# A three-part fp32 network on one core: weight blocks summed on VectorE, their parts stored as they are decoded, low halves taken one operation later, output stores on ScalarE's queue

## The chip, the cores and the metric

One Trainium2 chip, one of its cores. The engines are TensorE (PE; its weight loads PEld), VectorE (DVE), ScalarE (ACT), GpSimd (POOL) and SyncE (SP), which here only issues transfers. The metric is the device time of one execution in microseconds (us).

## The reference

With N = 3072 tokens of width 384, three parts run one after the other, all in fp32:

```python
state = alpha * state + outer(k_t, v_t); y_t = q_t @ state      # 4 x 8 heads, 768 steps
x = y as 3072 x 384
for tokens with x @ w_skip > 0: x += gate * (max(x @ w1[e], 0) @ w2[e])   # one of 8 experts
h = maximum(maximum(x @ w1, x @ w2), x @ w3)                    # 3 x (384 -> 768)
out = h @ w_out                                                 # 768 -> 384
```

## The kernel before

All fp32 products run as three matmuls of halves: each number is split in a high half h and a low half l = t - h, and the product is hh + hl + lh (fp32r operands). The change lies in the last part, the dense stage, which starts 299.7 us into the profiled execution, and in how its weights are made ready while the experts run.

**Decoding.** The four weights of the dense stage arrive as 64-bit words in 12 units of 128x768 (weight w, third u, in the order `ORDER`). `mdecs` decodes a unit on ACT (L98) and DVE (L108, L109, L102, L103, in place in a buffer `dt`), casts the high half `mh` on ACT (L612) and subtracts the low half `ml` (L615) on POOL for the first seven units, on DVE for the others. The last units, the u = 2 thirds of w = 0, 1, 2, are decoded in the first rounds of the dense stage.

**Token groups.** The tokens stand in six groups of 512. Groups 0 and 1 are computed directly, in six rounds each, f = 0 to 5 (128 columns of the hidden layer): `gemm1(g, f)` is 27 matmuls of 128x512 into three banks; ACT copies the first bank to `hf` (L841), DVE takes the maximum with the two others (L844), ACT casts the high half (`hb0h`/`hb1h`) and POOL subtracts the low half (`hb0l`/`hb1l`). `gemm2` of the round before (12 matmuls of 128x384) follows. Its last round copies four banks to `ob` on ACT (L862, a ring of three) and stores each (L863).

**Jobs.** The other four groups use a scheme of 15 block products in place of 18, for which sums of weight blocks and of token blocks are needed. `sums(w)` adds mh + ml back into whole blocks `tb` on POOL (L874, 128x768) and stores the parts of seven single blocks (`ONE`) as they are to the scratch `wd` in DRAM (L877). `wjobs` makes 13 combinations of blocks on DVE (L882), casts the high half of eight of them on ACT (L888), subtracts the low half on DVE (L889) and stores both to `wd` (L890). `xjobs(s)` transposes the token groups (`xg`, loaded by L815, transposed on PE at L820, copied to `temps` by ACT, L920/L997), makes 12 combinations on DVE (L906 to L910), and 15 high and low halves (L927 on ACT; L928 on POOL for the six of `XPOOL`, else on DVE). `pump(g, f, n)` emits the next n jobs behind a bank, so that jobs and rounds share the engines' queues:

```python
                if w == 0:
                    A.copy(t, ph)
                    pump(g, f, 2)
                else:
                    V.tensor_tensor(t, ph, t, ALU.max)
                    pump(g, f, 1)
```

**Steps.** Then two passes s = 0, 1 follow, each of six `step`s of 15 products (L970 to L972, 45 matmuls of 128x512) with weights reloaded from `wd` (`wdload`, L955 and L956), and a round of `outs2` and `store`, beside which the token blocks of the second pass are made.

**Order.** Each engine runs its instructions in the order of the program. Loads of `xg`, stores to `wd` and stores of the output all stand in SP's queue, in that order too: an issue that waits holds all behind it.

Of the kernel before, what the change touches and what calls it, by code (L numbers as in the profile page):

```python
# [55 lines left out]
GT = 512  # L56
# [3 lines left out]
LOADAT = 4  # L60
# [11 lines left out]
XSEQ = ((3, (2, 0), 1, (2, 1), 1), (6, (1, 0), 1, (2, 0), 1), (0, (0, 0), 1, 6, 1), 0, (9, 0, 1, (2, 1), 1), 9,  # L72
# [3 lines left out]
XPOOL = (7, 13, 3, 14, 2, 6)  # L76
# [5 lines left out]
def tile_gla_moe_moe2(ctx, tc, akq, vp, rp, wgt, cst, io, ew, md, out):  # L82
# [37 lines left out]
    with tc.manual_schedule():  # L120
# [465 lines left out]

        def mload(i):
            rm[i] = rmp.tile([128, 2 * UN], F32, name="rm")
            w, u = ORDER[i]
            SY.dma_start(out=rm[i].bitcast(I32), in_=md[3 * w + u].bitcast(I32))  # L590

        def mdecs():

            ts = {}

            def begin(i):
                if i < len(ORDER):
                    if i + 1 < len(ORDER):
                        mload(i + 1)
# [203 lines left out]
        wd = tc.dram_tile([nf2, 128, NR * 256], F32, name="wd")  # L803
        wv = wd.rearrange("f p (r t c) -> r p f t c", r=NR, t=2)
# [17 lines left out]
        def gemm1(g, f):  # L822
# [13 lines left out]
            for w in range(3):  # L836
# [12 lines left out]
        def gemm2(g, f):  # L849
# [4 lines left out]
            for c in range(4):  # L854
# [14 lines left out]
        mv = lambda m, w, k: m[w].rearrange("p (f k c) -> k p f c", f=nf2, k=k3)[k]  # L869
        fv = lambda a: a.rearrange("p (f c) -> p f c", f=nf2)  # L870
# [41 lines left out]
        def xjobs(s):  # L912
            reads = lambda j: [XONE.get(j, j)] if isinstance(j, int) else [j[1], j[3]]
            last = {v: i for i, j in enumerate(XSEQ) for v in reads(j)}
            free, at = list(temps), {}
            for k, n in ((1, 0), (2, 0), (2, 1), (0, 0), (0, 1), (1, 1)):
# [4 lines left out]
                if s == 0:  # L921
                    yield
            for i, j in enumerate(XSEQ):
                src = [at[v] for v in reads(j)]
                free[:0] = [at.pop(v) for v in reads(j) if last[v] == i]
# [8 lines left out]
                yield  # L934
# [6 lines left out]
        jobs = alljobs()  # L941
# [35 lines left out]
        def step(i):  # L977
# [26 lines left out]
            if i:  # L1004
                wdload(i + 1)
            neg(t5, p("A", 7))
            next(tail, None)
# [9 lines left out]
            sub(t3, p("D", 4))  # L1017
            lmax(t3, t1)
            add(t2, p("A", 5))
# [5 lines left out]
            def rest():  # L1025
                V.scalar_tensor_tensor(t2, p("A", 12), -1.0, t2, ALU.mult, ALU.max)
# [16 lines left out]
        def store(s, n, c, po, last=False):  # L1043
# [5 lines left out]
            else:  # L1049
                ends["A"] = A.copy(o, po)  # L1050
            ends["S"] = SY.dma_start(out=out[r0:r0 + 128, :], in_=o)

        pend = None
        for g in range(ng):
            for f in range(nf2):
# [3 lines left out]
                if g == 0:  # L1059
# [4 lines left out]
                    if 1 <= f < 4:  # L1064
                        sums(f - 1)
# [15 lines left out]
        gemm2(*pend)  # L1081
        wdload(1)
# [247 lines left out]
```

## Time and profile before

| | us |
|---|---|
| median of 3 runs (lowest, highest) | 622.01 (621.72, 623.18) |
| profiled execution, its own time | 624.9 |
| span of its profile | 623.1 |
| PE busy | 578.6 (93%) |
| DVE busy | 454.9 (73%) |
| ACT busy | 295.3 (47%) |
| POOL busy | 281.3 (45%) |
| mean granted TensorE clock, share of full | 0.976 |

The trace is of one execution. Times in its rows are microseconds from the span's start. Durations in a timeline overlap the next start a little, since an engine starts the next instruction before the last has fully ended; the distance of two starts is what one costs in a row. "[3.81 <-DVE xhl L118]" is idle time of the engine just before the instruction, and what ended it.

### The profile page before, as it was taken

To read this page: it belongs to the slowest core of one execution; us is meant where nothing else is said; L and a number is where in the kernel's file an instruction comes from. 1 tells how busy PE (TensorE), PEld (TensorE's weight loads), DVE (VectorE), ACT (ScalarE), POOL (GpSimd) and SP (SyncE) were. 2 spreads that over 40 slices of the span, in tenths; PEclk is the share of its full clock that TensorE was granted. 3 is DMA by queue.
4 is the path that set the end of the run, shared out by engine and by line. 5 is a ranking of instruction groups with operands and counts; after the bars stand their busy time and mean duration, and the time that the engine had idled before them with its cause. 6 is when DMAs were issued, how large, how long until landed. Compare 5 with 4: busy or idle time off the path is not lost. (4 is left out here: it accounts for less than half of the span.)

```text
span 623.1 us, 10650 instructions
## 1 busy us (share of the span) xinstructions
PE 578.6 (93%) x3995; PEld 510.4 (82%) x3995; DVE 454.9 (73%) x726; ACT 295.3 (47%) x593; POOL 281.3 (45%) x223
## 2 busy tenths in 40 slices
PE   7999999979999999999997975997999998999996
PEld 4888888869899999999786864786777798777795
DVE  7899999956898889898698953365676856686710
ACT  3555575644666666663323233244445355535411
POOL 6453788534355655543267310153445324445310
PEclk9999999999999999999997996998999999999999
DMA  8789997733768766744087267202846441746011
GB/s 326 290 244 329 318 337 267 292 117 116 271 256 300 246 237 230 277 180 170 27 268 230 102 213 275 94 2 72 332 158 220 138 157 42 275 145 228 7 53 56
DMA packets 50524, 123.03 MB, mean 197 GB/s; under 512 B 4098, under 2 KB 38384, under 8 KB 46880
## 3 DMA queue, kind: packets, MB, share of 16 engines
q1 hardware_dynamic: 47904, 117.43, 54.5%
q0 software_dynamic: 2560, 4.83, 2.0%
q8 instruction: 33, 0.54, 0.3%
q14 instruction: 27, 0.22, 0.1%
HBM read 93.03 MB, written 32.28 MB: 201 GB/s over the span
## 5 line engine op out<-in xcount | busy, mean ns | idle before, releaser
L118 POOL TENSOR_TENSOR wl<-raw,wh 128x768 fp32r<-128x768 f32 x26 | 51.1, 1964 | 57.4 <-ACT wh L117 57.3
L118 DVE TENSOR_TENSOR wl<-raw,wh 128x768 fp32r<-128x768 f32 x38 | 56.3, 1481 | 10.4 <-ACT wh L117 10.4
L117 ACT CAST wh<-raw 128x768 fp32r<-128x768 f32 x64 | 53.4, 835 | 19.7 <-PE po L665 15.5
L645 PE MATMUL ph<-xh,wh 128*128 128x256 f32 x192 | 56.4, 294 | 0.6 <-DVE hl L651 0.5
L646 PE MATMUL ph<-xl,wh 128*128 128x256 f32 x192 | 54.4, 284 | 0.4 <-DVE xl L118 0.3
L647 PE MATMUL ph<-xh,wl 128*128 128x256 f32 x192 | 54.4, 283 | 0.0
L665 PE MATMUL po<-wh,hl 128*128 128x384 f32 x128 | 43.4, 339 | 1.2 <-DVE hl L651 1.2
L663 PE MATMUL po<-wh,hh 128*128 128x384 f32 x128 | 43.5, 340 | 0.0
L664 PE MATMUL po<-wl,hh 128*128 128x384 f32 x128 | 43.1, 337 | 0.0
L225 POOL TENSOR_TENSOR k<-akq,sf 128x512 f32<-128x512 f32 x24 | 28.5, 1186 | 24.5 <-DVE sf L222 16.0
L265 PE MATMUL ps<-q,k 64*128 64x128 f32 x384 | 32.1, 287 | 7.9 <-POOL q L240 3.4
L416 POOL DMA_INDIRECT slots<-xr,si x24 | 24.3, 1014 | 30.7 <-DVE xr L413 15.5
L645 PEld LDWEIGHTS ph<-xh,wh 128*128 128x128 f32 x192 | 36.6, 190 | 1.5 <-DVE hl L651 1.3
L646 PEld LDWEIGHTS ph<-xl,wh 128*128 128x128 f32 x192 | 36.4, 190 | 0.8 <-DVE xl L118 0.5
L265 PEld LDWEIGHTS ps<-q,k 64*128 64x128 f32 x384 | 26.4, 188 | 12.3 <-issue 4.8
L647 PEld LDWEIGHTS ph<-xh,wl 128*128 128x128 f32 x192 | 36.4, 189 | 0.0
L271 DVE TENSOR_TENSOR sm<-ps,cs 128x512 f32<-128x512 f32 x48 | 30.3, 674 | 3.5 <-remote 3.1
L651 DVE SCALAR_TENSOR_TENSOR hl<-ph,hh 128x256 fp32r<-128x256 f32 x64 | 26.2, 416 | 8.1 <-ACT hh L650 6.9
L236 DVE TENSOR_TENSOR_SCAN ap<-akq,pcs 128x521 f32<-128x521 f32 x24 | 29.8, 1241 | 2.2
L222 DVE TENSOR_TENSOR_SCAN sf<-akq,pcs 128x520 f32<-128x520 f32 x24 | 29.4, 1224 | 2.5 <-DMA akq<-in_akq_dram 2.2
L650 ACT ACTIVATE hh<-ph 128x256 fp32r<-128x256 f32 x64 | 24.6, 385 | 13.5 <-PE ph L647 12.2
L240 POOL TENSOR_TENSOR q<-akq,ap 128x512 f32<-128x512 f32 x24 | 28.4, 1183 | 4.9 <-DVE ap L236 2.9
(659 smaller groups left out, 1786.1 us busy)
## 6 DMA issues: line engine op xcount, KB each, us to landing
raw<-in_ew_dram SPq DMA_DIRECT2D x15, 1536.0 KB
akq<-in_akq_dram SPq DMA_DIRECT2D x22, 772.5 KB
rm<-in_md_dram SPq DMA_DIRECT2D x12, 768.0 KB
mh<-wd SPq DMA_DIRECT2D x7, 1024.0 KB
ml<-wd SPq DMA_DIRECT2D x7, 896.0 KB
raw<-wd SPq DMA_DIRECT2D x6, 1024.0 KB
raw<-wd SPq DMA_DIRECT2D x6, 896.0 KB
vt<-in_vp_dram SPq DMA_DIRECT2D x24, 200.0 KB
```

The lines of the kernel that those rows point to most:

```text
L117: A.copy(h, src)
L118: (eng or V).tensor_tensor(l, src, h.bitcast(F32), ALU.subtract)
L222: V.tensor_tensor_scan(sf[:, KW - 2::-1], al[:, KW - 1:0:-1], eb[:, KW - 1:0:-1], 0.0, ALU.mult, ALU.max)
L236: V.tensor_tensor_scan(ap, al, eb, 0.0, ALU.mult, ALU.max)
L265: T.matmul(ps[i][:, p, :], kh[j][r0:r0 + 64, p, :], qh[j][r0:r0 + 64, p, :], start=True, stop=True)
L271: V.tensor_tensor(t, fr[j][i], cmask[:, None, :].to_broadcast([128, NP, C]), ALU.mult)
L645: T.matmul(ph, wh[:, z], xh_[e][:, k, :], start=(k == 0), stop=False)
L646: T.matmul(ph, wh[:, z], xl_[e][:, k, :], start=False, stop=False)
L647: T.matmul(ph, wl[:, z], xh_[e][:, k, :], start=False, stop=(k == k3 - 1))
L663: T.matmul(po, hh[:, zm], wh, start=(f == 0), stop=False)
L664: T.matmul(po, hh[:, zm], wl, start=False, stop=False)
L665: T.matmul(po, hl[:, zm], wh, start=False, stop=(f == nf1 - 1))
```

## The change

1. `sums` runs on DVE, on two thirds of each block (128x512); the last third is copied by ACT out of the decode buffer when that third is decoded. It is a job (`yield`) like the others.
2. The parts of the seven `ONE` blocks are stored in thirds by `mdecs`, right behind the subtraction that makes the low half: 42 stores of 128x2x128 in place of 14 of 128x6x128, most of them during the experts.
3. Low halves, of weight combinations and of token blocks, are taken one operation (or more) after the cast of their high half, all on DVE; `XPOOL` is gone.
4. `pump` takes a time in place of a count: each job yields a cost, and jobs are emitted until the amount is spent.
5. Stores of the output go to ACT's queue, but for the last.
6. `wdload(0)` comes a round earlier; `gemm2` of the last round stands inside the first step, behind its fourth product; `add(t2, p("A", 5))` stands ahead of `lmax(t3, t1)` in each step.

```diff
-LOADAT = 4
+LOADAT = 3
+PUMP = (2.0, 1.3, 1.3, 2.0)
...
-XPOOL = (7, 13, 3, 14, 2, 6)
...
                 (G if i < EARLY else V).tensor_tensor(l, t, h.bitcast(F32), ALU.subtract)
+                for k in range(k3 if w < 3 else 0):
+                    if (w, k) in ONE:
+                        for j, m in enumerate((mh, ml)):
+                            SY.dma_start(out=wv[ONE[w, k]][:, 2 * u:2 * u + 2, j],
+                                         in_=mv(m[w], k)[:, 2 * u:2 * u + 2].bitcast(F32))
+                    if u == 2:
+                        A.copy(fv(blk[w, k])[:, 4:], t.rearrange("p (f k c) -> k p f c", f=2, k=k3)[k])
                 yield
...
                 if w == 0:
                     A.copy(t, ph)
-                    pump(g, f, 2)
+                    pump(PUMP[0] if g or f > 3 else 0.7)
                 else:
                     V.tensor_tensor(t, ph, t, ALU.max)
-                    pump(g, f, 1)
+                    pump(PUMP[w] if g or f > 3 else 0.7)
...
-                    SY.dma_start(out=out[g * GT + c * 128:g * GT + (c + 1) * 128, :], in_=o)
-
-        blk = {}
+                    A.dma_start(out=out[g * GT + c * 128:g * GT + (c + 1) * 128, :], in_=o)
+
...
-        def sums(w):
-            for k in range(k3):
-                G.tensor_tensor(fv(blk[w, k]), mv(mh, w, k).bitcast(F32), mv(ml, w, k).bitcast(F32), ALU.add)
-                if (w, k) in ONE:
-                    for t, m in enumerate((mh, ml)):
-                        SY.dma_start(out=wv[ONE[w, k]][:, :, t], in_=mv(m, w, k).bitcast(F32))
+        def sums():
+            for w, k in TORD:
+                V.tensor_tensor(fv(blk[w, k])[:, 0:4], mv(mh[w], k)[:, 0:4].bitcast(F32),
+                                mv(ml[w], k)[:, 0:4].bitcast(F32), ALU.add)
+                yield 0.7
 
         def wjobs():
-            ncl = 0
+            ncl, rest = 0, []
+
+            def low():
+                d, cl, r = rest.pop()
+                V.tensor_tensor(rs_(cl[:, :, 1]), fv(blk[d]), cl[:, :, 0], ALU.subtract)
+                SY.dma_start(out=wv[r], in_=cl)
+
             for d, a, op, b, r in WSEQ:
                 V.tensor_tensor(blk[d], blk[a], blk[b], op)
-                yield
-                if r is None:
-                    continue
-                cl = (rmt + clt)[ncl % 4].rearrange("p (f t c) -> p f t c", f=nf2, t=2)
-                ncl += 1
-                A.copy(rs_(cl[:, :, 0]), fv(blk[d]))
-                V.tensor_tensor(rs_(cl[:, :, 1]), fv(blk[d]), cl[:, :, 0], ALU.subtract)
-                SY.dma_start(out=wv[r], in_=cl)
-                yield
+                yield 0.95
+                if rest:
+                    low()
+                    yield 0.95
+                if r is not None:
+                    cl = (rmt + clt)[ncl % 4].rearrange("p (f t c) -> p f t c", f=nf2, t=2)
+                    ncl += 1
+                    A.copy(rs_(cl[:, :, 0]), fv(blk[d]))
+                    rest.append((d, cl, r))
+            low()
+            yield 0.95
...
+            def low():
+                j, v, t = rest.pop(0)
+                V.tensor_tensor(lo[j], t, hi[j].bitcast(F32), ALU.subtract)
+                if v is not None:
+                    free.append(t)
...
                 if isinstance(j, int):
                     A.copy(hi[j], src[0])
-                    (G if j in XPOOL else V).tensor_tensor(lo[j], src[0], hi[j].bitcast(F32), ALU.subtract)
-                    if j in XPOOL:
-                        continue
-                else:
-                    at[j[0]] = free.pop(0)
-                    comb(at[j[0]], src[0], j[2], src[1], j[4])
-                yield
+                    rest.append((j, at.pop(dead[0]) if dead else None, src[0]))
+                    continue
+                busy = lambda: any(r[2] is at[v] for r in rest for v in dead)
+                while len(rest) > 1 or busy() or rest and not (free or dead):
+                    low()
+                    yield 0.7
...
-        def pump(g, f, n):
-            if g or f > 3:
-                for _ in range(n):
-                    next(jobs, None)
+        def pump(us):
+            debt[0] += us
+            while debt[0] > 0:
+                c = next(jobs, None)
+                debt[0] = 0.0 if c is None else debt[0] - c
...
-            if i:
-                wdload(i + 1)
+            wdload(i + 1)
             neg(t5, p("A", 7))
+            if not i:
+                gemm2(*pend)
...
             sub(t3, p("D", 4))
+            add(t2, p("A", 5))
             lmax(t3, t1)
-            add(t2, p("A", 5))
...
-                ends["A"] = A.copy(o, po)
-            ends["S"] = SY.dma_start(out=out[r0:r0 + 128, :], in_=o)
+                A.copy(o, po)
+            st = (SY if last else A).dma_start(out=out[r0:r0 + 128, :], in_=o)
...
-                    pump(g, f, 2)
+                    pump(PUMP[3] if g or f > 3 else 0)
...
-        gemm2(*pend)
-        wdload(1)
```

The rows below are the program's instructions of one engine in order, before and after. First DVE in round f = 4 of group 0, from the decode of the last third of weight 2 (rm, dt, ml) to the round's split of the next group's transposed tokens (xhl). Before:

```order
L844 TENSOR_TENSOR hf_4204<-ph,hf_4204 128x512 x2
L108 SCALAR_TENSOR_TENSOR dt<-rm,dt 128x768
L109 SCALAR_TENSOR_TENSOR dt<-rm,dt 128x768
L615 TENSOR_TENSOR ml_2221<-dt,mh_2217 128x768
L102 TENSOR_SCALAR dt<-dt 128x768
L103 TENSOR_SCALAR dt<-dt 128x768
L118 TENSOR_TENSOR xhl_4199<-pt,xhl_4198 128x512
```

After:

```order
L881 TENSOR_TENSOR tb_4221<-mh_2217,ml_2221 128x512
L855 TENSOR_TENSOR hf_4233<-ph,hf_4233 128x512
L881 TENSOR_TENSOR tb_4221<-mh_2215,ml_2219 128x512
L855 TENSOR_TENSOR hf_4233<-ph,hf_4233 128x512
L881 TENSOR_TENSOR tb_4222<-mh_2216,ml_2220 128x512
L108 SCALAR_TENSOR_TENSOR dt<-rm,dt 128x768
L109 SCALAR_TENSOR_TENSOR dt<-rm,dt 128x768
L621 TENSOR_TENSOR ml_2221<-dt,mh_2217 128x768
L102 TENSOR_SCALAR dt<-dt 128x768
L103 TENSOR_SCALAR dt<-dt 128x768
L118 TENSOR_TENSOR xhl_4228<-pt,xhl_4227 128x512
```

The sums (L881) now stand between DVE's own operations ahead of the split; before, they were POOL's. Next SP's queue around the loads of the token groups (xg), in group 1. Before:

```order
L890 DMA wd<-cl_4195 128x6x256
L890 DMA wd<-rm 128x6x256
L815 DMA xg_4196<-x_63 128x4x384
L815 DMA xg_4197<-x_63 128x4x384
L863 DMA out_dram<-ob 128x384 x4
L890 DMA wd<-rm 128x6x256
L890 DMA wd<-cl_4194 128x6x256
```

After:

```order
L891 DMA wd<-cl_4224 128x6x256
L891 DMA wd<-rm 128x6x256 x2
L826 DMA xg_4225<-x_63 128x4x384
L826 DMA xg_4226<-x_63 128x4x384
L891 DMA wd<-cl_4223 128x6x256
L891 DMA wd<-cl_4224 128x6x256
```

The four output stores are gone from the queue, and one more store of a weight combination (the sixth of eight) stands ahead of the token loads. Last PE behind the last round of group 1. Before:

```order
L859 MATMUL po_4711<-mh_2218,hb0l 128x384
L857 MATMUL po_4708<-mh_2218,hb1h 128x384
L858 MATMUL po_4708<-ml_2222,hb1h 128x384
L859 MATMUL po_4708<-mh_2218,hb1l 128x384
...
L859 MATMUL po_4711<-mh_2218,hb1l 128x384
L970 MATMUL ph<-dt,raw 128x512
```

After:

```order
L870 MATMUL po_4779<-mh_2218,hb0l 128x384
L1000 MATMUL ph<-dt,raw 128x512
...
L1000 MATMUL ph<-rm,raw 128x512
L1001 MATMUL ph<-rm,raw 128x512
L1002 MATMUL ph<-rm,raw 128x512
L868 MATMUL po_4776<-mh_2218,hb1h 128x384
```

The product with hb1h and hb1l now comes after twelve matmuls of the first step.

## Rows read from the trace of the kernel before

**Rows 1.** View by windows, whole core: PE, PEld, DVE, ACT, POOL busy (x instructions), PEclk, DMA, GB/s

```profile
299.70:331.40 31.70, 31.70 (x149) 26.73 (x147) 24.98 (x24) 9.86 (x15) 17.08 (x10) 1.00 0.59 185
...
335.50:341.10 5.60, 5.60 (x15) 4.56 (x16) 4.56 (x5) 1.96 (x4) 3.46 (x2) 0.50 0.69 204
...
364.00:399.90 35.90, 24.89 (x103) 19.73 (x103) 12.80 (x17) 11.10 (x19) 2.98 (x3) 0.81 0.69 241
...
424.60:432.60 8.00, 4.10 (x15) 3.46 (x14) 4.63 (x7) 3.28 (x6) 1.71 (x2) 0.83 0.10 39
```

**Rows 2.** PE's waits from 290 to 623: us in total, times, longest us

```profile
PE pt L820 <- ACT tb L920: 7.1, 3, 5.3
...
PE pt L820 <- DVE xhl L118: 3.8, 1, 3.8
...
PE po L857 <- ACT hb1h L117: 2.7, 1, 2.7
...
PE ph L970 <- ACT tb L997: 1.9, 1, 1.9
```

**Rows 3.** Timeline of DVE: start, us, form [idle before <-releaser]

```profile
305.52 1.49 DVE L844 TENSOR_TENSOR hf<-ph,hf 128x512 f32<-128x512 f32 x2 [3.31 <-PE ph L829]
...
310.82 0.96 DVE L615 TENSOR_TENSOR ml<-dt,mh 128x768 fp32r<-128x768 f32 x1 [0.90 <-ACT mh L612]
...
311.70 0.55 DVE L102 TENSOR_SCALAR dt<-dt 128x768 f32<-128x768 f32 x1
...
325.17 0.95 DVE L108 SCALAR_TENSOR_TENSOR dt<-rm,dt 128x768 int32<-128x768 int32 x1
...
326.15 2.00 DVE L109 SCALAR_TENSOR_TENSOR dt<-rm,dt 128x768 int32<-128x768 int32 x1
...
330.60 2.18 DVE L102 TENSOR_SCALAR dt<-dt 128x768 f32<-128x768 f32 x1
...
334.77 0.68 DVE L118 TENSOR_TENSOR xhl<-pt,xhl 128x512 fp32r<-128x512 f32 x1
```

**Rows 4.** Timeline of POOL in the same stretch

```profile
326.05 1.29 POOL L118 TENSOR_TENSOR hb0l<-hf,hb0h 128x512 fp32r<-128x512 f32 x1 [2.61 <-ACT hb0h L117]
...
327.30 7.14 POOL L874 TENSOR_TENSOR tb<-mh,ml 128x768 f32<-128x768 f32 x3
```

**Rows 5.** Timeline of SP's queue, issues

```profile
367.74 1.73 SPq L815 DMA_DIRECT2D xg<-x  x2
...
369.56 8.08 SPq L863 DMA_DIRECT2D out_dram<-ob  x4
```

**Rows 6.** Timeline of ACT

```profile
376.80 0.48 ACT L862 COPY ob<-po 128x384 f32<-128x384 f32 x1 [7.15 <-DMA out_dram<-ob]
```

**Rows 7.** Timeline of DVE: two operations of 128x512 in a row

```profile
415.33 0.68 DVE L844 TENSOR_TENSOR hf<-ph,hf 128x512 f32<-128x512 f32 x1
...
415.93 0.68 DVE L910 TENSOR_TENSOR tb<-tb 128x512 f32<-128x512 f32 x1
```

**Rows 8.** Timeline of PE in the dense stage

```profile
374.19 0.63 PE L820 MATMUL pt<-cs,xg 128*128 128x128 f32 x4 [3.79 <-DMA xg<-x]
...
414.33 0.33 PE L857 MATMUL po<-mh,hb1h 128*128 128x384 f32 x1
...
422.60 0.33 PE L857 MATMUL po<-mh,hb0h 128*128 128x384 f32 x1
```

**Rows 9.** Timeline of PE, end of one step, start of the next

```profile
453.58 0.39 PE L971 MATMUL ph<-dt,raw 128*128 128x512 f32 x1
...
453.81 0.39 PE L972 MATMUL ph<-dt,raw 128*128 128x512 f32 x1
...
454.38 0.50 PE L970 MATMUL po<-ml,ml 128*128 128x512 f32 x1 [0.18 <-DVE tb L986]
```

**Rows 10.** ACT's wait on loads, 165 to 296; all L877 stores: count, min/median/max ns

```profile
ACT wh L117 <- DMA raw<-in_ew_dram: 3.1, 3, 1.4
...
L877 SPq DMA_DIRECT2D wd<-mh x7: 922/1185/1317, 317.5 to 333.5; - x7
```

More of the change, by code (lines that the diff above doesn't have):

```diff
@@ L71 @@
 XONE = {10: (2, 1), 11: (1, 0), 14: (0, 1)}
-XSEQ = ((3, (2, 0), 1, (2, 1), 1), (6, (1, 0), 1, (2, 0), 1), (0, (0, 0), 1, 6, 1), 0, (9, 0, 1, (2, 1), 1), 9,
[2 rows of a table removed]
+XSEQ = ((3, (2, 0), 1, (2, 1), 1), 3, (6, (1, 0), 1, (2, 0), 1), (0, (0, 0), 1, 6, 1), 0, (9, 0, 1, (2, 1), 1), 9,
[2 rows of a table added]
         (5, (0, 0), 1, (0, 1), 1), 5, (12, (0, 0), 1, (1, 0), 1), 12)
-XPOOL = (7, 13, 3, 14, 2, 6)
 K_LO = 2.0 ** -15
@@ L585, in tile_gla_moe_moe2 @@
         rm = {}
+        wd = tc.dram_tile([nf2, 128, NR * 256], F32, name="wd")
+        wv = wd.rearrange("f p (r t c) -> r p f t c", r=NR, t=2)
+        mv = lambda m, k: m.rearrange("p (f k c) -> k p f c", f=nf2, k=k3)[k]
+        fv = lambda a: a.rearrange("p (f c) -> p f c", f=nf2)
+        blk = {}
         def mload(i):
@@ L802, in tile_gla_moe_moe2 @@
         cut = lambda t, n=3: [t[:, i * GT:(i + 1) * GT] for i in range(n)]
-        wd = tc.dram_tile([nf2, 128, NR * 256], F32, name="wd")
-        wv = wd.rearrange("f p (r t c) -> r p f t c", r=NR, t=2)
         h_ = {}
@@ L862, in gemm2 @@
                     A.copy(o, po)
-                    SY.dma_start(out=out[g * GT + c * 128:g * GT + (c + 1) * 128, :], in_=o)
-        blk = {}
+                    A.dma_start(out=out[g * GT + c * 128:g * GT + (c + 1) * 128, :], in_=o)
         for i, (w, k) in enumerate(TORD):
             blk[w, k] = tb[i // 2][:, i % 2 * UN:(i % 2 + 1) * UN]
-        mv = lambda m, w, k: m[w].rearrange("p (f k c) -> k p f c", f=nf2, k=k3)[k]
-        fv = lambda a: a.rearrange("p (f c) -> p f c", f=nf2)
-        def sums(w):
-            for k in range(k3):
-                G.tensor_tensor(fv(blk[w, k]), mv(mh, w, k).bitcast(F32), mv(ml, w, k).bitcast(F32), ALU.add)
-                if (w, k) in ONE:
-                    for t, m in enumerate((mh, ml)):
-                        SY.dma_start(out=wv[ONE[w, k]][:, :, t], in_=mv(m, w, k).bitcast(F32))
-        def wjobs():
-            ncl = 0
+        def sums():
[3 more added lines that the diff above has]
+                yield 0.7
+        def wjobs():
+            ncl, rest = 0, []
[3 more added lines that the diff above has]
+                SY.dma_start(out=wv[r], in_=cl)
             for d, a, op, b, r in WSEQ:
                 V.tensor_tensor(blk[d], blk[a], blk[b], op)
-                yield
-                if r is None:
-                    continue
-                cl = (rmt + clt)[ncl % 4].rearrange("p (f t c) -> p f t c", f=nf2, t=2)
-                ncl += 1
-                A.copy(rs_(cl[:, :, 0]), fv(blk[d]))
-                V.tensor_tensor(rs_(cl[:, :, 1]), fv(blk[d]), cl[:, :, 0], ALU.subtract)
-                SY.dma_start(out=wv[r], in_=cl)
-                yield
+                yield 0.95
[9 more added lines that the diff above has]
+            yield 0.95
         lo, hi = {}, {}
@@ L914, in xjobs @@
             last = {v: i for i, j in enumerate(XSEQ) for v in reads(j)}
-            free, at = list(temps), {}
+            free, at, rest = list(temps), {}, []
             for k, n in ((1, 0), (2, 0), (2, 1), (0, 0), (0, 1), (1, 1)):
@@ L921, in xjobs @@
                 if s == 0:
-                    yield
+                    yield 0.7
[4 more added lines that the diff above has]
+                    free.append(t)
             for i, j in enumerate(XSEQ):
                 src = [at[v] for v in reads(j)]
-                free[:0] = [at.pop(v) for v in reads(j) if last[v] == i]
+                dead = [v for v in reads(j) if last[v] == i]
                 if isinstance(j, int):
                     A.copy(hi[j], src[0])
-                    (G if j in XPOOL else V).tensor_tensor(lo[j], src[0], hi[j].bitcast(F32), ALU.subtract)
-                    if j in XPOOL:
-                        continue
-                else:
-                    at[j[0]] = free.pop(0)
-                    comb(at[j[0]], src[0], j[2], src[1], j[4])
-                yield
+                    rest.append((j, at.pop(dead[0]) if dead else None, src[0]))
[3 more added lines that the diff above has]
+                    low()
+                    yield 0.7
+                free[:0] = [at.pop(v) for v in dead]
+                at[j[0]] = free.pop(0)
+                comb(at[j[0]], src[0], j[2], src[1], j[4])
+                yield 0.7
+            while rest:
+                low()
+                yield 0.7
         def alljobs():
@@ L939, in alljobs @@
             yield from xjobs(0)
-        jobs = alljobs()
-        def pump(g, f, n):
-            if g or f > 3:
-                for _ in range(n):
-                    next(jobs, None)
+        debt = [0.0]
+        def pump(us):
[3 more added lines that the diff above has]
+                debt[0] = 0.0 if c is None else debt[0] - c
+        jobs = sums()
         wb = {}
@@ L1025, in rest @@
             def rest():
-                V.scalar_tensor_tensor(t2, p("A", 12), -1.0, t2, ALU.mult, ALU.max)
+                ends["V"] = V.scalar_tensor_tensor(t2, p("A", 12), -1.0, t2, ALU.mult, ALU.max)
                 yield
@@ L1049, in store @@
             else:
-                ends["A"] = A.copy(o, po)
-            ends["S"] = SY.dma_start(out=out[r0:r0 + 128, :], in_=o)
+                A.copy(o, po)
+            st = (SY if last else A).dma_start(out=out[r0:r0 + 128, :], in_=o)
+            if not last:
+                ends["A"] = st
         pend = None
@@ L1063, in tile_gla_moe_moe2 @@
                         rmt += [rmp.tile([128, 2 * UN], F32, name="rm") for _ in range(2)]
-                    if 1 <= f < 4:
-                        sums(f - 1)
+                        for _ in jobs:
+                            pass
+                        jobs, debt[0] = alljobs(), 0.0
                 if f == 0:
```

4 rows, old and new, of the table XSEQ are left out of this document.

## The prediction

> **What bounds the kernel now.** I read the page first: PE is busy 93% of the span, so a gain is PE time that is now lost. The view by windows shows where. From the start of the dense stage to its first decode trouble PE has no gap (31.70 busy of 31.70 [rows 1]); the loss lies in four places behind it. A round of `gemm1` and `gemm2` that nothing disturbs takes 8.27 us: from one `gemm2` start, 414.33, to the next, 422.60 [rows 8]. The stage up to the first step at 432.6 has 12 rounds and nine sets of four transposes (0.63 long at the low clock [rows 8]; I count 0.4 a set), so 99.2 + 3.6 = 102.8 us of work in 132.9: some 30 us are lost. The table of PE's waits and the timelines name the losses.
>
> *At 331.4.* PE waits 3.8 us for `xhl` from DVE [rows 2]. DVE issues `xhl` at 334.77, since the two operations ahead of it, L102 and L103, take about 2.1 us each; L102 took 0.55 alone and 2.18 here [rows 3], while POOL runs three `sums` for 7.14 us from 327.30 [rows 4]. Behind the wait PE runs 5.6 us at a granted clock of 0.50, which is 1.2 GHz [rows 1]: half of that is lost. Together 4.1 idle and 2.8 of clock, 6.9.
>
> *364.0 to 399.9.* Two rounds and six sets of transposes need 2 x 8.27 + 6 x 0.4 = 18.9 and take 35.9 us, PE busy only 24.9 of them and at a mean clock of 0.81 [rows 1]: 17 lost. First 3.79 for the load of `xg` [rows 8], issued at 367.74 behind the fifth `wd` store, so 6.4 us from issue to PE's start at 374.19 [rows 5, 8]. Then the copies of the transposed blocks (ACT `tb`): 7.1 us in three waits, 5.3 the longest [rows 2]. ACT stood 7.15 us before its fourth `ob` copy, until an output store had read the ring's buffer [rows 6]; these stores are the next in SP's queue, 8.08 us for four [rows 5].
>
> *424.6 to 432.6.* `gemm2` of the last round needs 8.27 less 27 matmuls at 0.23 [rows 9], 2.1 us, and the stretch takes 8.0 [rows 1]: 5.9 lost, to the cast of hb1h (2.7 of it [rows 2]), the low half behind it, and half clock.
>
> *Later.* One wait of 1.9 for a `tb` copy of the second pass [rows 2], with its ramp 2.0. And ten joins of steps like that at 453.81: the next start is 0.57 us later, where matmuls follow at 0.23 [rows 9]: about 0.3 each, the end of the step before waiting for bank and maximum, 2.7 in all.
>
> **The change, part by part.**
>
> *Sums on DVE.* Nine operations of 128x512. None of this shape with `mh`, `ml` is in the trace; the nearest is L910, 128x512 from two SBUF blocks, 0.68 long and 0.60 behind the operation before it [rows 7]. Nine cost 5.4 us of DVE. They take POOL off nine operations of some 2.4 (7.14 for three [rows 4]). L102 and L103 fall back from 2.1 to 0.55 each. POOL's hb split stays: 1.29 at 326.05, beside L109, which took 2.00 where L108 of the same shape just before took 0.95 [rows 3, 4]; so about 1.0 per round is still lost on DVE. A round of DVE is then: three sums 1.8, two maxima 1.2, two decode passes 1.95, the 0.9 wait for ACT's `mh`, the low half 0.88 (310.82 to 311.70), L102 and L103 1.1, 1.0 of POOL: 8.8 us beside a round of 8.27 + 0.4 = 8.7. DVE just keeps up; `xhl` comes about 1.1 late in place of 4.1, and I take no half clock behind so short a gap. Gain 3.0 + 2.8 = 5.8. Bounds: 6.9 if DVE is in time, 2.5 if a sum beside POOL costs 1.3 in place of 0.6 (three rounds, 2 us late each at first).
>
> Here the Trainium skill says more ("SBUF — State Buffer", section "Who interferes with whom"): a VectorE operation that reads two SBUF inputs and a GpSimd operation on SBUF block each other for a whole instruction, whichever began first. The trace agrees as far as L109's 2.00 goes; by that rule each sum that meets an hb split also waits up to its 1.29, which is what the lower bound of 2.5 takes.
>
> *The backlog on DVE and the token loads.* The loads of `xg` stand behind the sixth `wd` store in SP's queue now, before behind the fifth. That store waits for DVE's low half. From the second round's maxima at 305.5 [rows 3] to it DVE has 25 operations of 128x512 (0.60 each), 8 decode passes (0.97), 4 low halves of the decode (0.88), 3 pairs L102 and L103 (1.14), 18 operations of 128x768 for combinations and their low halves (0.88, as a low half of the decode [rows 3]), 4 waits for ACT (0.9) and 6 times 1.0 beside POOL: 15.0 + 7.8 + 3.5 + 3.4 + 15.8 + 3.6 + 6.0 = 55.1, so 360.6. With 6.4 us from issue to use the block is there at about 367.0. PE is at its first transpose at 374.19 - 3.79 - 5.8 = 364.6, less 18 matmuls x 0.23, since the transposes now stand behind the first nine of that round: 360.5. It waits 6.5; I add 3 for the three sets behind it that wait for copies one after another, and 3 of half clock: 12.5 lost in place of 17. Gain 4.5. Bounds: 13 if DVE is some 6 us earlier and the loads come in time; nothing if the fourth `ob` copy waits as before.
>
> *Output stores on ACT's queue.* SP's 8.08 us go; the fourth `ob` copy still waits for the first store of the ring of three, but that is issued at once, behind its copy. ACT has the cast for hb, four copies, then `cl`, `hf` and the `tb` copies behind it. Each issue takes ACT time too; no row shows one on ACT, on SP the two loads of `xg` took 0.87 each [rows 5]. The second such place lies in step 0, where the last round's copies stand ahead of ACT's step work: I take 1 us of loss, bounds 0 and 3.
>
> *Low halves later, on DVE.* A low half no longer stands right behind its cast; DVE's waits for ACT beside weight jobs go, and the six halves on POOL, beside which DVE slows, too. Six more operations on DVE, 3.6 us, lie in rounds 8.27 long with the two maxima of 1.2 and about 5 of jobs. The jobs end in round 4 of group 1 and the last round has none. The last `gemm2` stands behind four products of step 0, 12 x 0.23 = 2.8 us, which cover the cast and the low half. Gain 5.9; bounds 5.9 and 3, if hb1l comes late still.
>
> *Second pass and joins.* Jobs of the second pass no longer wait with their low halves: 2.0 gained (0 to 2.0). `add(t2)` stands ahead of the maximum, so that the bank that the next step's product needs is free sooner: 2.7 gained (1 to 2.7).
>
> *Stores in thirds.* 28 stores now stand among the raw loads of the expert weights in SP's queue, and wait for low halves. The whole ones took 0.92 to 1.32 us of issue [rows 10]; ACT already waits three times for these loads, at most 1.4 [rows 10], and PE does not show it. So the cover is at least 1.4 us a load. I take 0.5 lost, bounds 0 and 6.
>
> The sum: 5.8 + 4.5 + 5.9 + 2.0 + 2.7 - 1.0 - 0.5 = 19.4. The profiled execution took 624.9 (span 623.1), so it would take 605.5; the median of the runs is 2.9 lower than that execution, 622.0, and so 602.6, say 602. A difference of 0.3%, about 1.9 us, is what a measurement of this kernel can tell from none.
>
> **The rivals.**
>
> *More is gained.* If DVE is done some 6 us sooner, as with POOL's share of 6.0 gone, the loads arrive before PE needs them; of the 17 only some 4 stay, and the sum grows by 8: about 594. For it: DVE's rows next to an idle POOL are short [rows 3]. Against: the hb split remains, once a round.
>
> *Less is gained.* DVE falls behind in every round, since sums and decode stand ahead of the maxima that free PE's banks; or the wait of the fourth `ob` copy stays at 7.15 [rows 6], since the stores share the transfers' engines with the loads then under way (DMA share 0.69 [rows 1]). Then the second term falls to nothing, the first to 2.5, and 1 to 3 more go in step 0: 8 to 11 saved, about 612. What the Trainium skill says ("DMA: Bandwidth & Descriptors", "Rules for kernel authors") speaks for it: issuing on a second engine's queue brings no bandwidth, only issue time. No run here shows that yet.
>
> *Slower.* The stores in thirds hold up the raw loads of the experts. SP runs them in order; if a store's low half on POOL is ready after the load behind it is due, that load comes late by as much. Six units are decoded beside batches of the experts, each with four or six stores. From some 3.3 us lost per unit, 6 x 3.3 = 19.8, it eats the whole gain, and at 4 the time is 622.0 + 4.6, about 627. Against: a unit's stores take at most 6 x 1.3 us of SP's issue, and six units are spread over 130 us.
>
> *The change does not do what it says.* DVE is as late with the sums as POOL made it, and all four stalls stay in size: 620 to 622.
>
> **How the numbers follow.** Forecast, 595.5 to 608.5 around 602: 0.55. More gained, about 594 down to 590: 0.17. Less gained, 609 to 615: 0.18. Slower: 0.05. No effect: 0.05, of which 0.03 within 0.3%. Faster by over 0.3% is then 0.55 + 0.17 + 0.18 + 0.02 = 0.92. The range of 8 in 10 takes in the forecast and most of both its neighbours: 591 to 614.
>
> **What would show it.** Right: L102 and L103 at 0.55 on DVE; PE's wait for `xhl` under 1.5 us and no stretch at 0.50 behind it; one wait of PE of 4 to 8 us for `xg`, near 360; ACT's wait ahead of the fourth `ob` copy below 3; PE without a gap at the start of the steps, joins of 0.23. Wrong: sums longer than 1 us each; a wait of PE for `hf` maxima (banks) in the rounds; ACT waiting for raw loads more than three times in the experts, or that stage ending later; PE in step 0 waiting for ACT.

## The result and the profile after

The changed kernel takes 604.8 us at the median (602.96 to 606.74) beside 622.6 of before (now 621.72 to 625.0, four runs): ratio 0.9709, 95% interval 0.9664 to 0.9753, so 18 us or 2.9% faster. The prediction said 602 (591 to 614). The profiled execution has a span of 604.9, 18.2 below that of before.

The page of the changed kernel, span and PE:

```profile
span 604.9 us, 10708 instructions
...
PE 567.7 (94%) x3994; PEld 506.4 (84%) x3995; DVE 440.4 (73%) x747; ACT 297.2 (49%) x602; POOL 251.0 (42%) x202
```

The view by windows of the changed kernel, cut where PE's work changes: from the first matmul of `gemm1` to PE's wait for `xg`, to the first undisturbed `gemm2`, to the first step, to the end (columns as in [rows 1]):

```profile
299.04:359.81 60.77, 60.26 (x283) 50.66 (x281) 53.69 (x65) 23.31 (x40) 12.94 (x8) 1.00 0.40 129
359.81:391.83 32.02, 19.25 (x81) 15.61 (x82) 11.65 (x16) 10.55 (x19) 3.54 (x2) 0.73 0.68 230
391.83:418.74 26.91, 26.91 (x131) 23.62 (x130) 17.11 (x26) 10.28 (x18) 7.50 (x4) 1.00 0.24 90
418.74:604.90 186.16, 180.03 (x865) 154.59 (x864) 102.31 (x160) 82.11 (x149) 67.15 (x49) 0.99 0.41 145
```

Before, the way to the wait for `xg` had a wait of 3.8 for `xhl` [rows 2] and 5.6 us at half clock [rows 1]; now PE is busy 60.26 of 60.77 at full clock. The second row answers to 364.0 to 399.9 of [rows 1]: still a hole, PE busy 19.25 of 32.02, clock 0.73. The third row has no gap, and the `gemm2` that stood at the end with 5.9 us lost is in the fourth. PE's waits from 290 on, us in total, times, longest:

```profile
PE pt L831 <- DMA xg<-x: 8.7, 1, 8.7
...
PE pt L831 <- ACT tb L934: 4.1, 3, 2.8
...
PE pt L831 <- DVE xhl L118: 0.5, 1, 0.5
```

Beside [rows 2], `xhl` fell from 3.8 to 0.5, hb1h and the second pass's `tb` are gone, and the wait for `xg` rose from 3.8 to 8.7. DVE around the old stall, to hold beside [rows 3]:

```profile
317.06 1.93 DVE L109 SCALAR_TENSOR_TENSOR dt<-rm,dt 128x768 int32<-128x768 int32 x1
...
320.77 0.55 DVE L102 TENSOR_SCALAR dt<-dt 128x768 f32<-128x768 f32 x1
...
321.83 0.68 DVE L881 TENSOR_TENSOR tb<-mh,ml 128x512 f32<-128x512 f32 x1
...
330.85 0.69 DVE L118 TENSOR_TENSOR xhl<-pt,xhl 128x512 fp32r<-128x512 f32 x1 [0.17 <-ACT xhl L117]
```

L102 is back at 0.55 and a sum costs 0.68, 0.60 to the next start (321.83 to 322.44 for the next). L109 still takes 1.93 beside POOL's hb split. SP's queue, ACT and PE at the loads of `xg`, to hold beside [rows 5, 6, 8]:

```profile
357.90 2.69 SPq L891 DMA_DIRECT2D wd<-rm  x2
...
360.69 2.01 SPq L826 DMA_DIRECT2D xg<-x  x2
...
362.79 9.88 SPq L891 DMA_DIRECT2D wd<-cl  x2
```

```profile
361.37 0.47 ACT L873 COPY ob<-po 128x384 f32<-128x384 f32 x1
...
361.87 0.39 ACTq L874 DMA_DIRECT2D out_dram<-ob  x1
...
362.30 0.48 ACT L873 COPY ob<-po 128x384 f32<-128x384 f32 x1 [0.46 <-ACT ob L873]
...
369.23 0.48 ACT L873 COPY ob<-po 128x384 f32<-128x384 f32 x1 [5.22 <-DMA out_dram<-ob]
...
371.67 0.59 ACT L934 COPY tb<-pt 128x512 f32<-128x512 f32 x1
```

```profile
368.47 1.09 PE L831 MATMUL pt<-cs,xg 128*128 128x128 f32 x4 [8.66 <-DMA xg<-x]
```

The loads are issued at 360.69 (forecast 360.6) and PE starts on them at 368.47, 7.8 later. ACT issues each output store behind its copy; the fourth copy waits 5.22 for the first store, and the copies of the transposed blocks stand behind it.

**Where the time came from.** PE's timeline gives the parts of each profiled span: the experts (first transpose of their tokens to the first matmul of `gemm1`), the dense stage up to the first matmul of step 0, and the rest. In before and in `g2_before` the last `gemm2` (2.1 us of work) lies in the dense part, else in the rest.

| kernel | ahead of the experts | experts | dense | rest |
|---|---|---|---|---|
| before | 159.1 | 140.5 | 132.9 | 190.5 |
| changed | 155.0 | 144.0 | 119.7 | 186.2 |
| changed, again | 159.6 | 143.0 | 118.7 | 186.0 |
| one_whole | 159.8 | 141.4 | 119.2 | 186.0 |
| out_on_sp | 160.7 | 141.8 | 119.6 | 185.9 |
| xg_first | 158.4 | 144.4 | 114.4 | 186.0 |
| xg_ring | 159.2 | 145.0 | 114.5 | 186.1 |
| xg_ring_sp | 161.1 | 142.8 | 111.3 | 185.7 |
| sums_pool | 159.1 | 142.6 | 122.0 | 186.2 |
| g2_before | 159.2 | 143.7 | 122.3 | 186.3 |
| lmax_first | 153.3 | 143.7 | 119.2 | 191.0 |
| low_now | 154.6 | 142.5 | 121.9 | 191.2 |
| best | 153.6 | 141.9 | 110.6 | 185.8 |
| best_hb | 154.6 | 142.2 | 110.3 | 185.8 |

Ahead of the experts every kernel's engines have the same instructions in the same order, yet that part takes 153.3 to 161.1. The values fall in two groups. In nine profiles, that of before among them, DVE and ACT stand idle for 3.1 and 2.9 us at one place, until between 132 and 136, and the part takes 158.4 to 161.1; in the other five (the first of the changed kernel, lmax_first, low_now, best and best_hb) they do not, and it takes 153.3 to 155.0. In before:

```profile
133.62 1.29 DVE L271 TENSOR_TENSOR sm<-ps,cs 128x512 f32<-128x512 f32 x2 [3.08 <-remote]
```

"Remote" means that no instruction of this profile ended the wait; its cause stays open. No edit lies there, so some 4 of the 18.2 us between the two spans are not the change's, and the columns behind it are the ones to compare. The two last columns repeat within about 1 us in the two profiles of the changed kernel. With the 2.1 us put on one side, the dense stage gained 11.1 and 12.1 in these two, the rest 6.4 and 6.6, and the experts lost 3.5 and 2.5: 14.0 and 16.2 in all.

### The profile page after: what moved, and what is told of

Its sections match the earlier page's. It is cut to its first block, busy times and chain, and to the rows that moved or that the text cites. A ratio compares the mean times of both kernels' runs of the same rounds, so it can differ in the third digit from the quotient of the medians.

```text
span 604.9 us, 10708 instructions
## 1 busy us (share of the span) xinstructions
PE 567.7 (94%) x3994; PEld 506.4 (84%) x3995; DVE 440.4 (73%) x747; ACT 297.2 (49%) x602; POOL 251.0 (42%) x202
## 4 chain that ended last, share of the span: by engine, by line
PE 59%; DVE 19%; issue 7%; DMA 6%; POOL 4%; ACT 3%; SPq 0%; DVEq 0%; ACTq 0%; POOLq 0%
PE po L1000 3%; PE po L1001 3%; PE po L1002 3%; DMA xs<-slots 3%; PE ph L1000 3%; PE ph L1001 3%; PE ph L1002 3%; DVE ap L236 2%; DVE sf L222 2%; PE ph L658 2%; PE po L678 2%; PE po L676 2%; DVE wl L118 2%; PE po L677 2%; PE ph L659 2%
## 5 line engine op out<-in xcount | busy, mean ns | idle before, releaser
L118 DVE TENSOR_TENSOR wl<-raw,wh 128x768 fp32r<-128x768 f32 x38 | 58.8, 1546 | 10.8 <-ACT wh L117 10.8
L118 POOL TENSOR_TENSOR hb1l<-hf,hb1h 128x512 fp32r<-128x512 f32 x6 | 12.2, 2028 | 55.1 <-ACT hb1h L117 55.1
L664 DVE SCALAR_TENSOR_TENSOR hl<-ph,hh 128x256 fp32r<-128x256 f32 x64 | 26.4, 417 | 10.6 <-ACT hh L663 10.5
L855 DVE TENSOR_TENSOR hf<-ph,hf 128x512 f32<-128x512 f32 x24 | 16.5, 686 | 22.6 <-PE ph L840 22.5
```

What stands on the lines that cost most here:

```text
L118: (eng or V).tensor_tensor(l, src, h.bitcast(F32), ALU.subtract)
```

## The experiments

The kernels were run in four sets, whose times differ (before at 622.6, 627.1, 626.9 and 623.6), so each kernel is compared by its ratio to before in its own set; 0.001 of ratio is 0.62 us. The changed kernel **again** gave 609.27 beside 627.12, 0.9710 (0.9683 to 0.9737).

> The changed kernel once more, as the measure for the others. My theory: about 605, ratio to before 0.971; the stage up to the experts, whose instructions stand in the same order in both kernels, varies by some 4 us from one execution to the next, and PE's waits for hl in the expert stage (5.0 us after, 2.0 before) are an effect of the stores in thirds, so they come again. Rival: those waits vary as the first stage does, and this run shows 1 to 3 us of them.

The waits for `hl` came again, 3.5 us of them, above the 1 to 3 of the rival and below the 5.0 of the first profile. All ten profiles with stores in thirds have 3.1 to 5.4 us of them, the four without 1.7 to 2.9.

**one_whole.** The stores of the single blocks whole, behind the last third:

```diff
-                    if (w, k) in ONE:
+                    if u == 2 and (w, k) in ONE:
...
-                            SY.dma_start(out=wv[ONE[w, k]][:, 2 * u:2 * u + 2, j],
-                                         in_=mv(m[w], k)[:, 2 * u:2 * u + 2].bitcast(F32))
+                            SY.dma_start(out=wv[ONE[w, k]][:, :, j], in_=mv(m[w], k).bitcast(F32))
```

> The parts of the seven single blocks are stored whole, behind the last third of each weight, as before the change: no store among the raw loads of the experts. Theory: the stores in thirds make PE wait for hl in the expert stage (5.0 us against 2.0); without them the stage is 2 to 4 us shorter, and 14 stores of 384 KB crowd the dense stage a little: 1 to 3 us below the changed kernel. Rival: the waits vary by themselves: within 1 us of it, or above it since the stores now collide with others.

608.11, ratio 0.9685 (0.966 to 0.9711): 1.6 us below the changed kernel, but the intervals overlap. The traces say more. SP's queue of the changed kernel in the experts:

```profile
239.82 0.35 SPq L430 DMA_DIRECT2D raw<-in_ew_dram  x1
...
240.90 0.38 SPq L625 DMA_DIRECT2D wd<-mh  x1
...
247.94 0.38 SPq L625 DMA_DIRECT2D wd<-ml  x1
...
250.71 0.40 SPq L430 DMA_DIRECT2D raw<-in_ew_dram  x1
```

The store at 247.94 waits for its low half, and the raw load behind it is issued at 250.71; the one before stood at 239.82. ACT's wait on raw loads, changed kernel and then one_whole, to hold beside [rows 10]:

```profile
ACT wh L117 <- DMA raw<-in_ew_dram: 5.7, 2, 3.4
```

```profile
ACT wh L117 <- DMA raw<-in_ew_dram: 1.6, 2, 1.0
```

In all ten profiles with stores in thirds the longest such wait is 3.1 to 3.5 us; in the four without, 0.6 to 1.4. The experts take 141.8 to 145.0 with them (mean 143.3) and 140.5 to 142.2 without (141.5); the two ranges overlap by 0.4. The mechanism of the prediction's slower rival is there, at some 2 us in all in place of its 20 to 24.

**xg_first.** The loads of `xg` behind the second `wd` store of a combination:

```diff
-                if f == 0:
-                    for i in range(1 + g):
-                        xgload(i, 1 + g + i)
+                if f == 0 and g == 0:
+                    xgload(0, 1)
...
+                    if f == 4:
+                        xgload(0, 2)
+                        xgload(1, 3)
```

> The two loads of xg stand behind the second wd store of the weight combinations, not behind the sixth. Theory: the 17 us lost near 360 to 392 hang on the order in SP's queue behind DVE's backlog; PE's wait for xg (8.7) and part of the half clock go, ACT's wait of 5 us before the fourth ob copy stays: 8 to 12 us below the changed kernel, about 595. Rival: ACT's fourth ob copy is the next wait and holds the tb copies as long as the loads did: at most 4 us below, 601 or more. Second rival: the loads were late because the transfers' engines are full; then the wd stores come late in their place and nothing is gained.

605.2, ratio 0.9656 (0.963 to 0.9682): 3.4 us below, 4.8 in the dense column. The first rival holds. SP's queue, PE's wait and ACT:

```profile
351.13 1.73 SPq L826 DMA_DIRECT2D xg<-x  x2
```

```profile
PE pt L831 <- ACT tb L934: 9.3, 3, 8.0
```

```profile
365.11 0.47 ACT L873 COPY ob<-po 128x384 f32<-128x384 f32 x1
...
365.62 0.39 ACTq L874 DMA_DIRECT2D out_dram<-ob  x1
...
366.04 0.48 ACT L873 COPY ob<-po 128x384 f32<-128x384 f32 x1 [0.46 <-ACT ob L873]
...
368.94 0.48 ACT L873 COPY ob<-po 128x384 f32<-128x384 f32 x1 [1.26 <-DMA out_dram<-ob]
...
371.37 0.59 ACT L934 COPY tb<-pt 128x512 f32<-128x512 f32 x1
```

The loads are out at 351 and PE no longer waits for them, but 9.3 us for ACT, whose chain of copies and issues runs from 365.11 to 370: the issue of a store, 0.34 to 0.69 here, starts when its copy has ended, and the next copy starts 0.46 and more after that end.

**xg_ring** and **xg_ring_sp.** On top of xg_first, the fourth output copy of group 0 into a buffer of its own; and, in the second, all output stores on SP's queue:

```diff
-                    o = obuf()
+                    o = rmp.tile([128, UN], F32, name='dt')[:, 0:DM] if g == 0 and c == 3 else obuf()
...
-                    A.dma_start(out=out[g * GT + c * 128:g * GT + (c + 1) * 128, :], in_=o)
+                    SY.dma_start(out=out[g * GT + c * 128:g * GT + (c + 1) * 128, :], in_=o)
```

> xg_first, and the fourth output copy of group 0 goes to a buffer of its own in place of the ring's first. Theory: with the loads early, PE's wait of 8.0 for the tb copies is ACT's chain from 365.1 to 370.2: four output copies with an issue behind each, each issue waiting for its copy, and 1.26 before the fourth; only the 1.26 goes: 1 to 2 us below xg_first. Rival: the ring of three is the cause, and 4 us or more go.

> xg_ring with all output stores in SP's queue. Theory: issues on ACT cost ACT about 0.9 us a store (0.4 to 0.7 of issue, 0.5 of waiting for the copy just before); without them the four copies take 2 us in place of 5, PE's wait for tb falls to 4 or less: 3 to 5 us below xg_first. Rival: SP's queue holds the output stores behind wd stores as before the change, but the copies of group 0 no longer wait for them, so nothing is lost; the gain is under 1 us if ACT's issues were not on the path.

xg_ring: 604.22, 0.9642 (0.9618 to 0.9665), 1 us below xg_first with overlapping intervals, the dense column the same: the ring of three was not the cause. xg_ring_sp: 601.93, 0.9604 (0.9581 to 0.9626), 6.6 us below the changed kernel, dense 3.2 below xg_ring. ACT there:

```profile
366.19 1.23 ACT L873 COPY ob<-po 128x384 f32<-128x384 f32 x3
...
367.30 0.50 ACT L873 COPY dt<-po 128x384 f32<-128x384 f32 x1
...
368.88 0.63 ACT L934 COPY tb<-pt 128x512 f32<-128x512 f32 x1
```

Four copies take 1.5 us, and the first `tb` copy comes 2.7 us behind the first output copy, where it came 6.3 behind before (365.11 to 371.37 above). The theory holds: with the loads early, the issues on ACT were on the path. PE's longest wait for `tb` falls from 7.7 to 4.5, not to the 4 or less expected.

**out_on_sp.** All output stores back on SP's queue and nothing else:

```diff
-                    A.dma_start(out=out[g * GT + c * 128:g * GT + (c + 1) * 128, :], in_=o)
+                    SY.dma_start(out=out[g * GT + c * 128:g * GT + (c + 1) * 128, :], in_=o)
...
-            st = (SY if last else A).dma_start(out=out[r0:r0 + 128, :], in_=o)
+            ends["S"] = SY.dma_start(out=out[r0:r0 + 128, :], in_=o)
```

> All output stores back in SP's queue. Theory: little of the gain came from the queue; the first output store took 7.3 us on ACT's queue since the transfers' engines were full, so ACT waits there for 5 to 9 us and the time is 0 to 3 us above the changed kernel, 605 to 608. Rival: the queue was the cause of the stall of 17 us before the change, and SP's order costs 5 us or more: 610 or more.

610.83, ratio 0.9727 (0.97 to 0.9755), 1.1 above with intervals that overlap; dense the same. SP and ACT:

```profile
364.14 2.02 SPq L826 DMA_DIRECT2D xg<-x  x2
...
366.25 9.13 SPq L874 DMA_DIRECT2D out_dram<-ob  x4
```

```profile
374.55 0.48 ACT L873 COPY ob<-po 128x384 f32<-128x384 f32 x1 [8.49 <-DMA out_dram<-ob]
```

ACT's wait is 8.49 in place of 5.2, behind a load that is late in any case. So moving the stores gave nothing that stands clear of noise. The Trainium skill ("DMA: Bandwidth & Descriptors", "Rules for kernel authors") says that spreading transfers over several engines' queues doesn't help bandwidth and only saves issue time. These runs agree in so far as the time is the same within the intervals; what an issue takes on ACT is seen in xg_first.

**sums_pool.** The nine sums of 128x512 on POOL:

```diff
-                V.tensor_tensor(fv(blk[w, k])[:, 0:4], mv(mh[w], k)[:, 0:4].bitcast(F32),
+                G.tensor_tensor(fv(blk[w, k])[:, 0:4], mv(mh[w], k)[:, 0:4].bitcast(F32),
```

> The changed kernel with the nine sums of 128x512 on POOL. Theory: L102 and L103 on DVE go back to about 2 us each beside them, PE's wait for xhl comes back with some of the half clock behind it: 2 to 6 us above the changed kernel. Rival: DVE is rid of 5.4 us, so the wd stores and the loads of xg come earlier, and the time is the same or less.

610.96, ratio 0.9754 (0.9728 to 0.9779): 2.8 us above, dense +2.8. The size is the theory's, the place is not: DVE, POOL and PE's waits:

```profile
308.98 6.94 DVE L108 SCALAR_TENSOR_TENSOR dt<-rm,dt 128x768 int32<-128x768 int32 x1
...
315.95 0.96 DVE L109 SCALAR_TENSOR_TENSOR dt<-rm,dt 128x768 int32<-128x768 int32 x1
```

```profile
310.07 1.29 POOL L118 TENSOR_TENSOR hb0l<-hf,hb0h 128x512 fp32r<-128x512 f32 x1
...
311.31 3.78 POOL L881 TENSOR_TENSOR tb<-mh,ml 128x512 f32<-128x512 f32 x3
```

```profile
PE pt L831 <- DMA xg<-x: 6.6, 1, 6.6
...
PE ph L838 <- ACT hf L852: 3.5, 1, 3.5
```

L108, 0.95 alone, takes 6.94 while POOL has a split and three sums; ACT and PE then wait 3.5 for the bank. `xhl` is in time, and the loads come 2 us sooner for PE (6.6), as the rival said. From the first `gemm1` matmul to the wait for `xg`:

```profile
301.70:368.02 66.32, 62.84 (x283) 52.59 (x281) 58.06 (x59) 24.53 (x42) 24.73 (x18) 0.95 0.40 129
```

That is 66.3 us, where the changed kernel needs 60.8: on POOL the sums cost 5.5 there, and 2.7 of it come back behind, mostly from the shorter wait.

**g2_before.** The last `gemm2` ahead of the first step again:

```diff
-            if not i:
-                gemm2(*pend)
...
+        gemm2(*pend)
         hsl = [s_ for m in (mh[1], ml[1], mh[2], ml[2]) for s_ in cut(m, 4)[2:]]
```

> The changed kernel with the last gemm2 ahead of the first step again. Theory of the prediction: the wait for hb1h and hb1l and the half clock come back, 3 to 6 us above the changed kernel. Rival: the jobs end earlier now, so that ACT and POOL are free at that place (in the changed kernel the cast starts 0.1 us behind the maximum and the low half at 418.3); then only 0.5 to 1 us come back, and the gain of the last round is the earlier end of the jobs.

612.8, ratio 0.9773 (0.9749 to 0.9796): 3.9 us above, 3.3 of it in the two last columns. PE's waits:

```profile
PE ph L1000 <- ACT tb L1027: 2.3, 1, 2.3
...
PE po L870 <- POOL hb1l L118: 0.4, 1, 0.4
```

The low half costs 0.4, as the rival said; but the `gemm2`'s four output copies with their issues now stand ahead of step 0's own copies on ACT, and PE waits 2.3 for L1027. The place inside the step hides the copies, not only the cast. The waits of 2.7 and 1.2 that before had at this place, for the cast of hb1h and its low half, do not return without it: in before that cast stood on ACT behind casts of jobs, and no job is left there in the changed kernel.

**lmax_first.** The maximum of t3 ahead of the sum again:

```diff
-            add(t2, p("A", 5))
             lmax(t3, t1)
+            add(t2, p("A", 5))
```

> The changed kernel with the maximum of t3 ahead of add(t2, p(A, 5)) again. Theory: the joins of the steps lengthen from 0.23 to 0.5 to 0.6 again, ten times 0.3: 2 to 3 us above the changed kernel. Rival: the joins were short for another reason (copies in another order), and the time is within 1 us.

609.56, ratio 0.9777 (0.9759 to 0.9796): 4.2 us above, the rest +4.9. A join, on PE:

```profile
439.46 0.39 PE L1002 MATMUL ph<-dt,raw 128*128 128x512 f32 x1
...
440.04 0.50 PE L1000 MATMUL po<-ml,ml 128*128 128x512 f32 x1 [0.19 <-DVE tb L1016]
...
440.37 0.39 PE L1001 MATMUL po<-ml,ml 128*128 128x512 f32 x1
```

0.58 to the next start and 0.33 to the one behind, where 0.23 is usual: 0.45 lost. There are ten such joins, five in each pass; they lose 0.33 to 0.47 each, 4.3 together, and the same ten in before 4.0.

**low_now.** Low halves directly behind the casts, on DVE:

```diff
                     rest.append((j, at.pop(dead[0]) if dead else None, src[0]))
+                    low()
+                    yield 0.7
                     continue
```

(and in `wjobs`, behind `rest.append((d, cl, r))`).

> The changed kernel with each low half right behind the cast of its high half, still on DVE. Theory: DVE waits for ACT's cast at each of the low halves (about 0.9 each), six of them stand ahead of the loads of xg, and the jobs of both passes end later: 4 to 9 us above the changed kernel. Rival: DVE has room behind the loads, and only the six ahead of them count: 1 to 3 us above.

614.06, ratio 0.9839 (0.9819 to 0.9859): 8.1 us above; dense +2.6, the rest +5.1. PE's waits:

```profile
PE pt L831 <- DMA xg<-x: 13.8, 1, 13.8
...
PE ph L1002 <- ACT tb L1029: 4.4, 1, 4.4
```

Of the parts put back one by one, taking the low halves later is the largest: the `xg` wait is 13.8 in place of 8.7 without it, and 4.4 come back at the start of the second pass.

**best** and **best_hb.** xg_ring_sp with the edit of one_whole; and, in the second, on top of that:

```diff
-            split(hh, hl, t, G)
+            split(hh, hl, t, V)
             h_[g, f] = hh, hl
```

> xg_ring_sp with the single blocks stored whole again. Theory: as for the changed kernel, about 1 us less than xg_ring_sp, from the waits for hl in the expert stage: ratio to before 0.957 to 0.960. Rival: 14 stores of 384 KB now meet the earlier loads of xg, and nothing is gained or 1 us lost.

> The same with the low halves of hb on DVE in place of POOL. Theory of contention: each POOL split costs a DVE operation beside it about 1.0 us (L109 at 1.93 in place of 0.95), and one more operation of DVE costs 0.6: DVE is done 2 to 4 us earlier by the sixth wd store, and the kernel is 1 to 4 us faster than the last. Rival: DVE stands idle for the cast of hb in front of each split, 0.5 to 1 us a round, and the kernel is the same or 1 to 4 us slower.

best: 594.6, ratio 0.9536 (0.9518 to 0.9555), faster than before and than the changed kernel. Its page:

```profile
span 591.8 us, 10668 instructions
```

By the ratios that is 10.9 us below the changed kernel, and xg_ring_sp 6.6 of it. By the columns behind the first (mean of the changed kernel's two profiles) best is 10.5 below and xg_ring_sp 9.0, so that one_whole's edit brings 1.5 here (experts 0.9, dense 0.7), close to the 1.6 of its ratio alone; the ratio of xg_ring_sp, from another set of runs, shows 2.4 less than its columns, and why stays open. best_hb: 593.39, 0.9502 (0.948 to 0.9524), 2.1 us below best with intervals that overlap; its dense column is 0.3 lower. DVE there:

```profile
323.97 0.96 DVE L109 SCALAR_TENSOR_TENSOR dt<-rm,dt 128x768 int32<-128x768 int32 x1
...
330.80 0.69 DVE L118 TENSOR_TENSOR hb1l<-hf,hb1h 128x512 fp32r<-128x512 f32 x1 [0.69 <-ACT hb1h L117]
```

L109 is back at 0.96, but DVE stands idle for 0.69 before the split of a round without sums. Both effects are there; which is larger, these runs don't show.

## Why the prediction was right, and which step was not

The direction and the range were right. The sum, 19.4 forecast beside 18 measured, is closer than its terms: 4.5 of it came to nothing, other terms were off by 1 to 2 us either way, and the terms that can be followed in the profiles make 14.0 and 16.2. That the totals agree so well is in part luck. Of the signs that the prediction named, two missed: the wait for `xg` (8.7, named 4 to 8) and ACT's wait ahead of the fourth copy (5.2, named below 3); and one of its signs of being wrong is there, experts that take longer. Term by term:

- **Sums, `xhl`: 5.8.** From the first `gemm1` matmul to PE's wait for `xg` it is 60.8 us, and was 70.7 with 18 matmuls more (4.1): 5.8 gained, as forecast. sums_pool shows that the engine is the cause: with the sums on POOL 5.5 are lost again in this part, though at another wait. The Trainium skill ("SBUF — State Buffer", "Who interferes with whom") says that a VectorE instruction with two SBUF inputs contends with GpSimd instructions that read SBUF, and that the shared ports are locked exclusively. The trace agrees, and L108 there stood 6 us longer than alone under several POOL operations in a row, where the prediction's lower bound took one split of 1.29.
- **The backlog and the loads: 4.5, measured 0.** This is the step that failed: "I add 3 for the three sets behind it that wait for copies one after another, and 3 of half clock: 12.5 lost". The stretch from 359.81 to 391.83 takes 32.0 for 14.8 us of work (18 + 27 matmuls at 0.23, 12 of `gemm2`, six sets of transposes), 17.2 lost. DVE's end and the issue were right to 0.1 us; the landing took 7.8 in place of 6.4, so PE waited 8.7 and not 6.5; 4.1 went to the `tb` copies and 4.4 to the half clock, so 2.2, 1.1 and 1.4 more than the three parts of the term. Nothing of the 17 us of before was gained here. What it takes is shown by xg_first and xg_ring_sp: the loads ahead of the backlog bring 4.8 in the dense column, and the stores off ACT another 3.2. (The 0.63 that the prediction reads as a set of transposes at the low clock is one at full clock; at half clock a set takes 1.09. The sum hardly changes by it.)
- **Output stores on ACT: -1.** No gain shown for the queue (out_on_sp), and 3.2 us of cost once the loads are early (xg_ring against xg_ring_sp). The cost of an issue on ACT, which no row of before showed, is about 0.8 us a store: from the first of the four copies to the cast behind them it is 4.7 us in xg_ring and 1.5 in xg_ring_sp.
- **Last `gemm2`: 5.9.** No gap is left. Of the two reasons forecast, the earlier end of the jobs is the larger: with it alone (g2_before) 0.4 of waiting for the low half remains. The place inside the step, which was to cover cast and low half, covers ACT's output copies as well; without it 3.9 are lost, 2.3 of them waiting behind those copies and 0.4 for the low half, the rest open.
- **Second pass and joins: 4.7, measured 6.5.** The mechanism held, the joins were mis-sized: ten in before lose 4.0 and not 2.7. The rows give 0.34 a join and so 3.4, and the matmul behind the first is slow too (0.33). The wait of the second pass was 2.1 with its ramp, forecast 2.0; with the low halves taken at once (low_now) it is there again, with 4.4.
- **Stores in thirds: -0.5, measured about -2** (experts, 143.3 against 141.5 in the mean).

What stays open: the columns hold 14.0 and 16.2 of the 18 us, and the part ahead of the experts varies by more than the difference. The change also reorders the jobs of the token blocks (`XSEQ`), which its list does not name; that, and `pump` by time, have no run of their own.

## What to carry to other kernels

An in-order queue that carries stores waiting for compute should not have loads behind it: `xg` and the raw weights were both late for the store ahead of them. Moving the loads of `xg` forward took its wait away, and moving the thirds out from among the raw loads shortened theirs; moving the output stores to another engine did not help. Before a stall is priced as removed, follow the engine that comes next: behind the load stood ACT's chain of copies and issues, nearly as long. A low half that waits for another engine's cast is worth an operation's distance on an engine that runs in order: without it 8.1 us were lost here. And two spans are best compared from the first changed instruction on.

## What the runs showed of the hardware

- A DVE operation of 0.95 took 6.94 beside POOL operations in a row (sums_pool). It goes the other way too: POOL's split took 1.29 at its shortest, 1.81 to 2.09 in most rounds beside DVE's sums and combinations, and 4.13 beside a row of five DVE operations of 0.68 (changed kernel, at 402.29), behind whose end 1.16 of it lies.
- An output store of group 0 issued on ACT took 0.34 to 0.74 of issue, and the next copy started 0.46 to 0.77 after the last one's end where it waited for no buffer; copies in a row without issues follow 0.37 apart (xg_ring, xg_ring_sp).
- The part ahead of the experts, the same instructions in the same order, took 158.4 to 161.1 us in nine profiles and 153.3 to 155.0 in five; a wait of 3.1 us on DVE near 133, which no row explains, is there in the nine alone.
